# Asking later for the second group's weights, with two parts in flight instead of four

## The chip, the cores and the metric

The kernel runs on one core of a Trainium2 chip. The metric is device time in microseconds (us) for one execution. The engines named below are TensorE (PE, with its weight loads as PEld), VectorE (DVE), ScalarE (ACT), GpSimd (POOL) and SyncE (SP), which here only issues DMAs. Each engine works through its own instructions in program order.

## The reference

A retention layer, then a feed-forward block with the activation h * erf(softplus(h)):

```python
batch, n_heads, seq, head_dim = (8, 8, 576, 64)
scores = scale * np.matmul(q, k.transpose(0, 1, 3, 2))
Dmat = np.where(rel >= 0, gamma[:, None, None] ** rel[None, :, :], 0.0)
attn = np.matmul(scores * Dmat[None], v)
x = attn.transpose(0, 2, 1, 3).reshape(4608, 512)
h = x @ w_in                       # w_in  512 x 2048
sp = np.maximum(h, 0.0) + np.log1p(np.exp(-np.abs(h)))
out = (h * erf(sp)) @ w_out        # w_out 2048 x 512
```

The two weight matrices arrive as 64-bit floats. The kernel reads them as pairs of 32-bit words and rounds them to 32-bit floats itself.

## The kernel before

**Attention.** The 4608 tokens are cut into 36 pieces of 128 tokens, all eight heads at a time. A piece goes through three stages, `transposes` (L303), `scores` (L329) and `outputs` (L342); `attend` (L438) runs the next ones of the list. From piece 8 on, q and k are loaded as 32-row squares (`raw_qs`, `raw_ks`, four or eight DMAs each, L130) and turned by DVE into `qT` and `kT` (L314), which the scores on PE (L335) need. The squares have two buffers: `transposes(i)` asks for q and k of piece i+2, `outputs(i)` asks for the rows of k and v of piece i+3 (`raw_k`, `raw_v`, L144). All these DMAs are issued by SP.

**Feed-forward.** Four pieces make a chunk of 512 tokens, and there are nine chunks. The 2048 inner columns are cut into four groups of 512. That gives 36 pairs (group, chunk), numbered n = 0 to 35, the nine chunks of group 0 first. Both products of a pair are made in a seven-product scheme, so a pair has seven products of PE in `First` (x times w_in, L478) and seven in `Second` (times w_out, L585), besides the first pair, which is computed plainly (L532). Below, Fn and Sn are `firsts[n]` and `seconds[n]`.

**Order.** The main loop (L735) writes out the order of all engines by hand. Its blocks are F1, S0, F2, S1, F3, S2 and so on. Block Fn holds the three products of Fn's `middle`, the two of S(n-1)'s `first` and the two of Fn's `last`. Block Sn holds Sn's `middle` (3), F(n+2)'s `first` (2) and Sn's `last` (2). Between products stand attention stages and single steps of the weight rounding. `run(steps, rounds)` (L696) says how many rounding steps follow each product.

**Weights.** `load_weights` (L224) issues the next part: 128 partitions by 1024 words, 512 KB, as two DMAs of 256 KB for w_in or one of 512 KB for w_out, into one of the four `wraw` buffers. A group has four parts `wa` of w_in and four parts `wb` of w_out. `rounding` (L232) rounds one part in five steps:

1. ACT: absolute value of the high words into the operand tile, and the low words scaled (L246, L247)
2. DVE: a clamp (L251)
3. DVE: a shift (L255)
4. DVE: the sign put back (L259)
5. DVE: a mask (L264); then two operations on POOL (L266, L267), which replace two on DVE outside the first four parts; then, for groups after the first, the next `load_weights`

After the fourth part of `wa` and of `wb` come four more steps, one addition on DVE each (`sums_in`, `sums_out`). A group so takes 48 steps. `most_g` lets a step touch a group only from the group before it on. The operand tiles `wa` and `wb` have two buffers each. Group 1's `wa` is first used by F9's `first`, which stands in block S7, and its `wb` by S9's `first`, in block F10.

Before the change, two parts of group 1 are asked for at block F1 and two at block F2 (L739), so four are in flight, and each finished part asks for the next. Its rounding starts in block S0, with five steps in each block Fn and two in each Sn, and ends in block S6.

Of the kernel before, what the change touches and what calls it, by code (L numbers as in the profile page):

```python
# [54 lines left out]
def kernel(  # L55
# [15 lines left out]
    n_ch = n_tok // TCH  # L71
# [26 lines left out]
    def tt(out, in0, in1, op):  # L98
        nc.vector.tensor_tensor(out=out, in0=in0, in1=in1, op=op)  # L99
# [75 lines left out]
    A11, S3, A12, A22, S1, S2, S4 = range(7)  # L175
    B11, T3, B21, B22, T1, T2, T4 = range(7)
    weights = {}

    def operands(name, g):
        if (name, g) not in weights:  # L180
            shape = [P, 7, 2, GW] if name == "wa" else [P, 7, GP, OH]
            weights[name, g] = wpool.tile(shape, FP32, tag=name, name=name)
        return weights[name, g]
# [40 lines left out]
    def load_weights():  # L224
        part = next(coming, None)
        if part is not None:
            t = wraw.tile([P, 2 * WP], UINT32, tag="wraw", name="wraw")
            for rows, src in part[0]:
                nc.sync.dma_start(out=t[rows].rearrange("p (h f) -> p h f", h=2), in_=src)
            words.append((t, *part[1:]))  # L230

    def rounding():  # L232


        while True:
            while not words or words[0][2] > most_g[0]:
                yield
            t, name, g, slot, j, sums = words.pop(0)
            w = operands(name, g)
            dst = w[:, slot : slot + 2, j, :]  # L240
            pairs = t[:, :].rearrange("p (h f two) -> p h f two", h=2, two=2)
            pairs_f = t[:, :].bitcast(FP32).rearrange("p (h f two) -> p h f two", h=2, two=2)
            low, high = pairs[:, :, :, 0], pairs[:, :, :, 1]
            r_f, high_f = pairs_f[:, :, :, 0], pairs_f[:, :, :, 1]
            a_f, a = dst, dst.bitcast(UINT32)
            nc.scalar.activation(a_f, high_f, AF.Abs)  # L246
            nc.scalar.mul(out=r_f, in_=low, mul=2.0**-52)  # L247
            yield


            nc.vector.tensor_scalar(  # L251
                out=a_f, in0=a_f, scalar1=HIGH_LEAST, scalar2=HIGH_MOST, op0=ALU.max, op1=ALU.min
            )
            yield
            nc.vector.tensor_scalar(  # L255
                out=a, in0=a, scalar1=3, scalar2=0x3FFFFFFF, op0=ALU.logical_shift_left, op1=ALU.bitwise_and
            )
            yield
            nc.vector.scalar_tensor_tensor(  # L259
                out=a, in0=high, scalar=0xC0000000, in1=a, op0=ALU.bitwise_and, op1=ALU.bitwise_or  # L260
            )
            yield

            nc.vector.tensor_scalar(out=high, in0=a, scalar1=0xFF800000, scalar2=None, op0=ALU.bitwise_and)  # L264
            engine = nc.vector if (name, g) == ("wa", 0) else nc.gpsimd
            engine.tensor_tensor(out=r_f, in0=high_f, in1=r_f, op=ALU.mult)  # L266
            engine.tensor_tensor(out=a_f, in0=a_f, in1=r_f, op=ALU.add)  # L267
            if g > 0:
                load_weights()
            yield  # L270
            if sums:
                yield from sums(*(w[:, i] for i in range(7)))

    round_step = rounding()

    def round_weights(n=1):
        for _ in range(n):
            next(round_step, None)
# [155 lines left out]
    def after_chunk(c):  # L434

        return stages.index((outputs, (c + 1) * PC - 1)) + 1

    def attend(upto):  # L438
        while done[0] < min(upto, len(stages)):
            of, i = stages[done[0]]  # L440
            of(i)
            done[0] += 1
# [7 lines left out]
    def store_x(c):  # L450
        nc.sync.dma_start(out=xd[c], in_=x[0, c][:, :n_dc])

    def operands_x(g, c):
        t = x[g, c]
        b11, b12, b21, b22 = (t[:, 2 * d : 2 * d + 2, h * TH : (h + 1) * TH] for d in range(2) for h in range(2))
        t1, t2, t4 = (t[:, n_dc + j, :].rearrange("p (d i) -> p d i", d=2) for j in range(3))
        if g == 0 or c == 0:
            tt(t1, b12, b11, ALU.subtract)
            tt(t2, b22, t1, ALU.subtract)
            tt(b12, b22, b12, ALU.subtract)  # L460
        else:
            tt(t2, b12, b11, ALU.add)
            tt(t1, b22, t2, ALU.subtract)
        if g == 0:
            store_x(c)
        tt(t4, b21, t2, ALU.subtract)
        x[g, c] = {A11: b11, A12: b21, S4: b22, A22: t4, S1: t1, S2: t2, S3: b12}

    class First:
# [3 lines left out]
            self.g, self.c = g, c  # L473

        def product(self, a, acc, start):
            for j in range(GP):
                for d in range(2):
                    nc.tensor.matmul(  # L478
                        acc[:, j * TH : (j + 1) * TH],
                        lhsT=weights["wa", self.g][:, a, d, j * P : (j + 1) * P],  # L480
                        rhs=x[self.g, self.c][a][:, d, :],
                        start=(start and j == 0 and d == 0),
                        stop=(d == 1),
                        skip_group_check=True,
                    )
# [71 lines left out]
        def sums(self, parts=(0, 1)):  # L557
            g11, g21, g12, g22 = (t[:, j] for t in (self.t1, self.t2) for j in range(2))
            s1, s2, s3, s4 = (self.s[:, i, j] for i in range(2) for j in range(2))
            if 0 in parts:  # L560
                tt(s1, g12, g22, ALU.add)
                tt(s2, s1, g11, ALU.subtract)
            if 1 in parts:
                tt(s3, g11, g12, ALU.subtract)
                tt(s4, g21, s2, ALU.subtract)

            self.left = {B11: g11, B21: g21, T2: s2, T3: s3, T1: s1, B22: s4, T4: g22}

    class Second:
# [9 lines left out]
                nc.sync.dma_start(out=self.o, in_=od[self.c])  # L579

        def product(self, b, acc, start):
            left = self.of.left[b]
            for j in range(GP):
                for tp in range(2):
                    nc.tensor.matmul(  # L585
                        acc[:, tp, :],
                        lhsT=left[:, j * TH + tp * P : j * TH + (tp + 1) * P],
                        rhs=weights["wb", self.g][:, b, j, :],
                        start=(start and j == 0 and tp == 0),
                        stop=(j == GP - 1),  # L590
                        skip_group_check=True,
                    )
# [86 lines left out]
    firsts = [First(g, c) for g, c in order]  # L679
    seconds = [Second(f) for f in firsts]  # L680
# [15 lines left out]
    def run(steps, rounds=(), stages=1):  # L696

        for step, _ in enumerate(steps):
            attend(min(done[0] + stages, most[0]))
            round_weights(rounds[step] if step < len(rounds) else 0)  # L700
# [34 lines left out]
    for b, nxt in zip(blocks[1:], blocks[2:] + [None]):  # L735
        n = order.index((b.g, b.c))
        if isinstance(b, First):
            most_g[0] = order[n - 1][0] + 1
            if n in (1, 2):  # L739
                load_weights()  # L740
                load_weights()
            run(b.middle(), (1, 1))
            firsts[n - 1].sums()
            run(seconds[n - 1].first(), (1, 1) if n > 1 else ())
            run(b.last(), (1,) if 1 < n < n_ch else ())
            most[0] = before_chunk(n + 3)
        elif n + 2 < n_s:
            f = firsts[n + 1]
            for step, _ in enumerate(b.middle()):
                attend(min(done[0] + 1, most[0]))  # L750
                if step == 0:
                    f.erf()
                elif step == 1 and n + 2 >= n_ch:
                    operands_x(*order[n + 2])
            if n + 2 < n_ch:
                attend(after_chunk(n + 2))
                operands_x(*order[n + 2])
            run(nxt.first(), (1,))
            f.multiply()
            seconds[n + 1].begin()  # L760
            if n_ch <= n + 3 < n_s:
                load_x(*order[n + 3])
            run(b.last(), (0, 1))
        elif n + 1 < n_s:
            firsts[n + 1].erf()
            seconds[n + 1].begin()
            rest = b.rest()
            for _ in range(3):
                next(rest)
            firsts[n + 1].multiply()  # L770
            run(rest)
            firsts[n + 1].sums((0,))
            first = nxt.first()
            next(first)
            firsts[n + 1].sums((1,))
            run(first)
        else:
            run(b.rest())
# [30 lines left out]
```

## Time and profile before

| | |
|---|---|
| time, median of 6 runs | 1038.26 us (1037.45 to 1038.70) |
| time of the profiled execution | 1038.08 us |
| its span, first to last instruction | 1036.3 us |
| mean granted TensorE clock | 0.998 |
| PE busy / PEld busy | 1016.5 us / 875.1 us |
| DVE / ACT / POOL busy | 675.2 / 387.5 / 125.6 us |
| DMA bytes, mean rate | 167.27 MB, 161 GB/s |

The profiled execution is one of the runs of the median; the 1.8 us by which its time exceeds its span lie before its first and after its last instruction. Busy time of PE includes modelled ends, so that 98% busy doesn't mean PE at its peak; a stall is seen where PE's busy time falls below the length of a window. The scores of the first pieces that use the squares stand at 67 us, those of the last piece at 320 us. Where a number below is the start of an instruction, it is in us from the start of the span.

These are the first products of some blocks on PE, to find the places in the trace:

| first product of | start, us |
|---|---|
| S0 first / F1 last | 80.1 / 88.2 |
| F2 middle / F2 last | 114.9 / 129.0 |
| F3 middle / F3 last | 156.2 / 169.4 |
| F4 first / F4 middle | 188.2 / 198.9 |
| F7 middle / F8 middle | 318.0 / 345.5 |
| F9 first / F9 middle | 363.6 / 370.5 |
| S9 first | 400.0 |

### The profile page before, as it was taken

The page shows a single profiled execution, that of the slowest core. Times are in us where ns is not written, and L with a number is a line of the kernel's source. Part 1 is how long each engine was busy: PE and PEld are TensorE (multiplying, and loading weights), DVE is VectorE, ACT ScalarE, POOL GpSimd, SP SyncE. Part 2 cuts the span into 40 slices and gives each one's busy share as a digit, 9 for nine tenths or more (in the row PEclk, how much of TensorE's full clock was granted, in tenths as well). Part 3 has the DMA queues.
Part 4 walks back from the last instruction along what each step waited for, and adds up shares of the span by engine and source line. Part 5 has one row for each costly group of instructions (what it writes and reads, how often), then busy time and mean ns, then how long its engine had stood idle before and what let it go on. Part 6 is the DMA issues. An engine that isn't in the chain of part 4 may idle for free.

```text
span 1036.3 us, 15904 instructions
## 1 busy us (share of the span) xinstructions
PE 1016.5 (98%) x6322; PEld 875.1 (84%) x6322; DVE 675.2 (65%) x1063; ACT 387.5 (37%) x477; POOL 125.6 (12%) x122
## 2 busy tenths in 40 slices
PE   9899999999999999999999999999999999999998
PEld 7777877778788888888888888888888888888887
DVE  3998967768876645567665656666666655555555
ACT  2353232232343444433434334444443333333332
POOL 2151222321312100100001000100100000000000
PEclk9999999999999999999999999999999999999999
DMA  9989989979984531633274424353333334444433
GB/s 192 203 208 225 252 183 250 226 182 250 225 198 141 182 123 40 240 146 142 65 260 143 168 96 143 143 214 152 122 122 122 122 121 130 132 131 131 127 88 116
DMA packets 148778, 167.27 MB, mean 161 GB/s; under 512 B 97632, under 2 KB 123360, under 8 KB 140640
## 3 DMA queue, kind: packets, MB, share of 16 engines
q1 hardware_dynamic: 147696, 165.47, 56.1%
q8 instruction: 50, 0.82, 0.3%
q10 hardware_dynamic: 1008, 0.79, 0.3%
q14 instruction: 24, 0.20, 0.1%
HBM read 119.02 MB, written 47.19 MB: 160 GB/s over the span
## 4 chain that ended last, share of the span: by engine, by line
PE 81%; DMA 8%; DVE 6%; SPq 3%; issue 1%; ACT 1%; POOL 0%; DVEq 0%; POOLq 0%
PE a L585 22%; PE a L478 21%; PE g L585 11%; PE g L478 11%; PE e L585 5%; PE e L478 5%; DMA raw_ks<-in_k_dram 2%; PE s L335 2%; PE o L353 2%; DMA raw_k<-in_k_dram 2%; SPq L130 1%; DVE t L99 1%; DMA od<-o 1%; SPq L144 1%; DVE x L99 1%; PE o L376 1%
## 5 line engine op out<-in xcount | busy, mean ns | idle before, releaser
L478 PE MATMUL a<-x,wa 128*128 128x256 f32 x1120 | 266.2, 381 | 0.0
L478 PEld LDWEIGHTS a<-x,wa 128*128 128x128 f32 x1120 | 211.7, 190 | 29.3
L585 PE MATMUL a<-wb,s 128*128 128x256 f32 x864 | 205.7, 381 | 0.0
L585 PEld LDWEIGHTS a<-wb,s 128*128 128x128 f32 x864 | 163.1, 190 | 23.4 <-ACT o L599 0.7
L99 DVE TENSOR_TENSOR t<-g,t 128x512 f32<-128x512 f32 x70 | 48.3, 690 | 151.5 <-ACT t L508 113.3
L478 PE MATMUL g<-x,wa 128*128 128x256 f32 x560 | 133.2, 381 | 0.5 <-DVE o L99 0.5
L478 PEld LDWEIGHTS g<-x,wa 128*128 128x128 f32 x560 | 105.8, 190 | 15.6 <-DVE o L99 0.9
L99 DVE TENSOR_TENSOR o<-a,o 128x512 f32<-128x512 f32 x108 | 74.3, 688 | 50.4 <-PE a L585 50.4
L503 ACT COPY t<-a 128x512 f32<-128x512 f32 x35 | 20.5, 586 | 187.5 <-PE a L478 187.5
L99 DVE TENSOR_TENSOR t<-t,s 128x1024 f32<-128x1024 f32 x72 | 88.1, 1264 | 0.0
L266 POOL TENSOR_TENSOR wraw<-wraw 128x512 f32<-128x512 f32 x28 | 29.4, 1051 | 463.5 <-DVE wraw L264 253.9
L547 ACT ACTIVATE s<-t 128x1024 f32<-128x1024 f32 x72 | 72.1, 1048 | 35.5 <-DVE t L99 35.5
L99 DVE TENSOR_TENSOR x<-x 128x512 f32<-128x512 f32 x116 | 77.9, 704 | 1.2
L514 ACT COPY t<-a 128x512 f32<-128x512 f32 x35 | 20.5, 586 | 153.0 <-PE a L478 153.0
L551 ACT ACTIVATE s<-s 128x1024 f32<-128x1024 f32 x72 | 72.1, 1049 | 0.4
L585 PE MATMUL g<-wb,s 128*128 128x256 f32 x288 | 68.6, 381 | 2.3 <-DVE t L99 2.3
L585 PE MATMUL a<-wb,t 128*128 128x256 f32 x288 | 68.6, 381 | 1.1 <-DVE t L99 1.1
L585 PE MATMUL e<-wb,t 128*128 128x256 f32 x288 | 68.6, 381 | 0.0
L585 PE MATMUL g<-wb,t 128*128 128x256 f32 x288 | 68.2, 380 | 0.0
L478 PE MATMUL e<-x,wa 128*128 128x256 f32 x280 | 66.8, 381 | 0.0
L99 DVE TENSOR_TENSOR o<-g,o 128x512 f32<-128x512 f32 x72 | 49.3, 685 | 25.6 <-ACT o L599 20.8
L585 PEld LDWEIGHTS g<-wb,s 128*128 128x128 f32 x288 | 54.3, 190 | 9.9 <-DVE t L99 2.5
(75 smaller groups left out, 1194.6 us busy)
## 6 DMA issues: line engine op xcount, KB each, us to landing
od<-o SPq DMA_DIRECT2D x54, 512.0 KB, 3.3
x<-xd SPq DMA_DIRECT2D x27, 1024.0 KB, 4.9
o<-od SPq DMA_DIRECT2D x27, 1024.0 KB, 4.9
raw_qs<-in_q_dram SPq DMA_DIRECT2D x96, 112.0 KB, 4.8
raw_ks<-in_k_dram SPq DMA_DIRECT2D x96, 112.0 KB, 4.2
xd<-x SPq DMA_DIRECT2D x9, 1024.0 KB, 5.2
raw_k<-in_k_dram SPq DMA_DIRECT2D x64, 128.0 KB, 4.5
raw_v<-in_v_dram SPq DMA_DIRECT2D x64, 128.0 KB, 4.3
```

The costliest lines, as they stand in the source:

```text
L99: nc.vector.tensor_tensor(out=out, in0=in0, in1=in1, op=op)
L130: nc.sync.dma_start(out=t[part * SQ : (part + 1) * SQ, :, at : at + m - SQ], in_=tokens[:, :, d0 : d0 + m - SQ])
L144: nc.sync.dma_start(out=t[r0 : r0 + n, e::2, :], in_=heads.rearrange("h p d -> p h d"))
L266: engine.tensor_tensor(out=r_f, in0=high_f, in1=r_f, op=ALU.mult)
L335: nc.tensor.matmul(ps[e][:, p, :], lhsT=t["kT"][heads[e], p, :], rhs=t["qT"][heads[e], p, :], start=True, stop=True)
L353: nc.tensor.matmul(o[p % 2][heads[(e + p) % 2], p // 2, :], lhsT=t["v"][:, 2 * p + e, :], rhs=t["sT"][:, e, p, :], start=(p < 2), stop=(no ...
L478: nc.tensor.matmul(acc[:, j * TH : (j + 1) * TH], lhsT=weights["wa", self.g][:, a, d, j * P : (j + 1) * P], rhs=x[self.g, self.c][a][:, d, :],
L503: nc.scalar.copy(out=self.t1[:, 1], in_=self.a)
L514: nc.scalar.copy(out=self.t2[:, 0], in_=self.a)
L547: nc.scalar.activation(self.s[:, j], t, AF.Softplus)
L551: nc.scalar.activation(self.s[:, j], self.s[:, j], AF.Erf)
L585: nc.tensor.matmul(acc[:, tp, :], lhsT=left[:, j * TH + tp * P : j * TH + (tp + 1) * P], rhs=weights["wb", self.g][:, b, j, :], start=(sta ...
```

## The change

Group 1's first part is asked for at the end of block F2 and another one at the end of block F3, one each. Each finished part still asks for the next one, so that about two are in flight from then on, through all later groups. Blocks S0, F2 and S1 lose their rounding steps. Blocks F3 on keep five and blocks S2 on two. Blocks S6 to S8 get a third one behind the last product of `middle`, as far as steps are left. Counted by steps: group 0 ends as before in F1; group 1's steps 1 to 24 (`wa`) run from F3 to F6, step 44 (the last part rounded) stands in S7, and steps 45 to 48 (the sums of `wb`) in F9. From group 2 on, the rounding steps stand where they stood. The order of PE's instructions is the same as before. The `rounded` set only serves assertions when the program is built.

```diff
+    rounded = set()
...
             if sums:
-                yield from sums(*(w[:, i] for i in range(7)))
+                for step, _ in enumerate(sums(*(w[:, i] for i in range(7)))):
+                    if step == 3:
+                        rounded.add((name, g))
+                    yield
...
         def product(self, a, acc, start):
+            assert ("wa", self.g) in rounded
...
         def product(self, b, acc, start):
+            assert ("wb", self.g) in rounded
...
             most_g[0] = order[n - 1][0] + 1
-            if n in (1, 2):
+            run(b.middle(), (1, 1) if n != 2 else ())
+            firsts[n - 1].sums()
+            run(seconds[n - 1].first(), (1, 1) if n > 2 else ())
+            run(b.last(), (1,) if 2 < n < n_ch else ())
+            if n in (2, 3):
                 load_weights()
-                load_weights()
-            run(b.middle(), (1, 1))
-            firsts[n - 1].sums()
-            run(seconds[n - 1].first(), (1, 1) if n > 1 else ())
-            run(b.last(), (1,) if 1 < n < n_ch else ())
             most[0] = before_chunk(n + 3)
         elif n + 2 < n_s:
...
                 elif step == 1 and n + 2 >= n_ch:
                     operands_x(*order[n + 2])
+                elif step == 2 and n_ch - 4 < n < n_ch:
+                    round_weights()
...
-            run(nxt.first(), (1,))
+            run(nxt.first(), (1,) if n > 1 else ())
             f.multiply()
...
-            run(b.last(), (0, 1))
+            run(b.last(), (0, 1) if n > 1 else ())
```

## The prediction, made before the run

> **What bounds the kernel now.** I read the share of each engine first, then the busy time by stretches, then what PE waited for, then SP's issues around those waits.
>
> ```profile
> PE 1016.5 (98%) x6322; PEld 875.1 (84%) x6322; DVE 675.2 (65%) x1063; ACT 387.5 (37%) x477; POOL 125.6 (12%) x122
> ...
> 84.00:133.00 49.00, 49.00 (x483) 40.02 (x480) 40.18 (x69) 15.42 (x20) 10.37 (x11) 1.00 1.04 228
> 133.00:177.00 44.00, 42.01 (x417) 34.05 (x417) 32.25 (x57) 12.30 (x16) 8.24 (x9) 1.00 0.95 214
> 177.00:214.00 37.00, 35.21 (x345) 28.65 (x342) 29.32 (x50) 10.43 (x14) 10.50 (x10) 1.00 1.05 240
> 214.00:262.00 48.00, 45.73 (x429) 37.45 (x426) 35.49 (x61) 14.20 (x19) 10.38 (x10) 1.00 0.86 205
> 262.00:316.00 54.00, 54.00 (x484) 44.09 (x486) 42.42 (x70) 20.67 (x27) 15.00 (x15) 1.00 0.94 205
> 316.00:350.00 34.00, 33.51 (x242) 28.33 (x239) 21.19 (x39) 12.76 (x17) 5.74 (x6) 1.00 0.44 140
> 350.00:1030.00 680.00, 680.00 (x3151) 598.77 (x3150) 410.08 (x615) 271.01 (x318) 38.23 (x33) 1.00 0.40 138
> ```
>
> Columns of the stretches: from and to, length, busy us of PE, PEld, DVE, ACT, POOL, granted clock, DMA share, GB/s. PE is the bound almost everywhere. From 350 us on it has no gap, so nothing can be gained there. Between 84 us, where the first load that the change moves is issued, and 350 us, PE lacks 1.99 + 1.79 + 2.27 + 0.49 = 6.54 us. That is the whole pot. The DMAs are busy at 0.86 to 1.05 until 316 us. What PE waited for in 84 to 350 us (total, times, longest):
>
> ```profile
> PE s L335 <- DVE kT L314: 3.8, 4, 1.8
> PE g L585 <- DVE t L99: 2.3, 2, 1.7
> PE g L478 <- DVE o L99: 0.5, 1, 0.5
> ```
>
> Four gaps before scores, waiting for turned k, make 3.8 us. One by one on PE's timeline they are 0.98 us at 140.86 (piece 16), 0.19 at 158.34 (18), 0.83 at 176.29 (20) and 1.79 at 187.06 (21). Behind the 1.8 stands this, on SP and in the chain of waits:
>
> ```profile
> 175.46 0.63 SPq L229 DMA_DIRECT2D wraw<-in_moe_w_out_dram  x1
> 176.19 1.99 SPq L130 DMA_DIRECT2D raw_qs<-in_q_dram  x4
> 178.27 3.65 SPq L130 DMA_DIRECT2D raw_ks<-in_k_dram  x4
> ...
> 187.87 1.81 SPq L130 DMA_DIRECT2D raw_ks<-in_k_dram  x4
> ```
>
> ```profile
> 175.46 6.13 DMA wraw<-in_moe_w_out_dram
> 181.59 0.02 issue
> 181.60 4.10 DMA raw_ks<-in_k_dram
> ```
>
> The same four issues of k take 3.65 us behind a weight part and 1.81 without one. The chain says why: the fourth waited until the weight part, eight DMAs before it in SP's order, had landed. A part costs the loads behind it twice, by bandwidth and by this wait. Piece 16 has the same picture:
>
> ```profile
> 125.72 2.60 SPq L229 DMA_DIRECT2D wraw<-in_moe_w_in_dram  x4
> 128.42 1.97 SPq L130 DMA_DIRECT2D raw_qs<-in_q_dram  x4
> 130.73 4.79 SPq L130 DMA_DIRECT2D raw_ks<-in_k_dram  x4
> ```
>
> **The change, part by part.** PE's order is unchanged and no instruction is added or dropped, so only gaps count. *Loads.* From 84 us to the end of the attention loads SP issued ten parts, and now issues six. Counted in the new order, the parts ahead of the q and k loads are: piece 16 four before, none now; pieces 18 and 20 five, then none and one; 21 six, one; 23 six, three; 25 seven, three; 33 nine, six. At 217 GB/s (the five stretches to 316 us, weighted) a part of 524288 bytes is 2.4 us. SP runs late in this stretch: the q squares of 21 could go out once piece 19's were turned at 163.7, and go out at 176.19. So five parts less, up to 12 us, is real lead for pieces 16 to 21, and the 3.79 us of their gaps should go. I take 3.6; at least 2.5, if 16 and half the rest go.
>
> *The two DVE gaps* (1.66 at 223.45 and 0.61 at 261.86) wait for an addition `t` that DVE reached late, since just before it had idled 2.04 + 1.43 us for q and k of piece 25, and 2.15 + 0.90 us for piece 29. With four parts less ahead, that idling shrinks by up to 9.6 us less the 3.8 that PE then runs earlier. I take 1.3 of the 2.27; bounds 0 and 2.27.
>
> *The gap at 347.88* (0.49) is DVE's queue, no DMA: behind the four operand sums stand a rounding step of 0.69 (L259), then the addition and two multiplications, and only then `o`, which frees the PSUM tile. Counting steps, that slot now holds an ACT step, and block S6's third step puts 0.42 (L264) earlier. Gain 0.2; bounds -0.4 and 0.49.
>
> *The moved steps.* S0, F2 and S1 lose nine steps, and S6 to F9 get them. In S7 the new steps are 0.42 (L255) and 0.69 (L259) on DVE, which idles 1.10 and 0.42 us there, at 367.35 and 370.73; cost nothing, 0.5 if that cover is gone. The weights' use is safe: step 24 falls in F6, 39 us before F9 needs it, and the sums end by 379 us, before S9's middle needs them at 407. POOL's two operations (1.04 + 1.29) come along, and POOL has 10 of 49 us busy. SP's waits at L229 for freed buffers (113.8 us for DVE after 350) go too, worth nothing where PE has no gap.
>
> *The new place.* Two parts, four DMAs of w_in, now stand between v of piece 22 and q of piece 23. SP reached that place at 191.91. At piece 16 the time from the first of four such DMAs to turned k was 125.72 to 140.80, 15.1 us. Piece 23's scores started at 204.11 without a gap, and will be wanted 3.8 us earlier, at 200.3. If SP is earlier by 3.8 only, the four go out at 188.1, k is ready at 203.2, and PE waits 2.9 us. If it is 7 us or more ahead, of the 12 that five parts give, PE waits nothing. I take the middle, 1.4; bounds 0 and 2.9.
>
> A load asked for late can also hold ACT: part 2's first step stands behind F4's first copy, at 190.18 + 0.59 before. With issue at 188.1 and 6.9 us to land (the four at 125.72 took 4.9 to 7.5), ACT stands until 195. Its next copy, at 196.07 before, had 5.30 us of idling ahead of it, and would be late by some 4 us, with DVE's clamp behind it by 2. I count that inside the same 2.9, as it is the same lateness.
>
> The trace shows the first two parts issued at 84.37 to 86.28, landed by 93.38 and first used at 105.53: they lie idle for 12 us, so there is room to ask later, and only part 2 comes near its use. The Trainium skill speaks against the change here: "DMA: Bandwidth & Descriptors", rules for kernel authors, says to issue a DMA early and wait for it late. By that rule alone asking later could only lose, and the sum would be zero or a loss.
>
> Sum: 3.6 + 1.3 + 0.2 - 1.4 = 3.7 us off the profiled execution's 1038.08 (span 1036.3 and 1.8 around it), that is 1034.4. The median of the runs is 0.18 higher than that execution, so 1034.6. Bounds: 3.79 + 2.27 + 0.49 = 6.55 gained, 1031.7; and 2.5 - 2.9 - 0.4 - 0.5 = 1.3 lost, 1039.6.
>
> **The rivals.** *All gaps go* (1031.7): five parts of lead outrun what PE gains, 12 us against 3.8, and at piece 23 three parts still do, 7.2 against 3.8. Against it: DVE is 72 to 82% busy there, and gaps closed early make later ones tighter.
>
> *The wait moves to piece 23* (about 1037.4): SP gets ahead only as far as PE does, because its other issues wait for buffers and results in order; 3.6 gained, 2.9 lost there, the rest unchanged. For it: the block of four is the very one that stalled piece 16. Against it: SP ran 12 us behind its buffers at piece 21.
>
> *Slower: the block of four arrives with no lead at all.* Issued at 191.9 it makes k of piece 23 ready at 207.0, 6.7 us after the wanted 200.3, and the late data carry the DVE gap at 223 along; 3.6 gained, 6.7 lost, 1038.26 + 3.1 = 1041.4. It decides once the issue comes later than 188.1 + 0.7 + 2.1 = 190.9, where loss exceeds gain by over 2.1. Against it: that needs five parts' transfers to have cost SP nothing, which the 3.65 against 1.81 denies.
>
> *It doesn't do what it says*: if attention loads, not weights, fill the DMAs to the same lateness, gaps stay, 1038. The rows of piece 21 speak against it; it belongs with no change.
>
> **How the numbers follow.** About 0.2%, 2.1 us, is what a measurement tells from no change: faster is below 1036.2, slower above 1040.3. Forecast (1034.6, own range 1032.6 to 1036.2) 0.42; all gaps go 0.20; moved to piece 23, or nothing done, 0.26; slower 0.12. That gives faster 0.62, same 0.26, slower 0.12. The range 1031.5 to 1038.8 leaves out the slower rival and the edge of no change.
>
> **What would show it.** Right: gaps at pieces 16, 20 and 21 gone; a gap of 0 to 2.9 at piece 23; PE busy 44.0 of 44 in the stretch that ends at 177; 350 on still without gaps. Wrong: gaps there in spite of four q and k issues at 1.8 us (then DVE was the cause), a long ACT wait at L246 for its part before F4's middle, or new gaps at S7 and F9.

## The result and the profile after

The changed kernel takes 1035.69 us (median of 18 runs, 1033.71 to 1038.21), beside 1038.47 for the kernel before (38 runs, those of the same chips included). The ratio is 0.9974, with a 95% interval of 0.9968 to 0.9981: faster by 0.26%, some 2.8 us. The forecast was 1034.6 us, with a range of 1031.5 to 1038.8, and faster with a chance of 0.62.

The profiled execution took 1036.4 us, with a span of 1034.6 us, 1.7 less than before. These are the same stretches of the changed kernel (from and to, length, busy us of PE, PEld, DVE, ACT, POOL, granted clock, DMA share, GB/s) and what PE waited for in 84 to 350 us (total, times, longest). Lines of the code have moved: the loads of weights are now L230, the turning L318, scores L339, the products L483 and L591, the mask of the rounding L265 and POOL's two operations L267 and L268.

```profile
133.00:177.00 44.00, 44.00 (x429) 35.90 (x428) 33.70 (x60) 14.25 (x19) 9.14 (x10) 1.00 0.88 209
177.00:214.00 37.00, 37.00 (x347) 30.25 (x347) 29.35 (x47) 11.57 (x17) 8.00 (x9) 1.00 1.04 228
214.00:262.00 48.00, 45.20 (x435) 36.83 (x434) 33.41 (x60) 16.24 (x22) 11.03 (x12) 1.00 0.88 204
262.00:316.00 54.00, 54.00 (x510) 44.18 (x509) 45.98 (x76) 15.81 (x21) 11.50 (x12) 1.00 0.97 220
316.00:350.00 34.00, 31.96 (x198) 27.12 (x197) 19.73 (x32) 14.04 (x20) 7.32 (x6) 1.00 0.35 117
350.00:1030.00 680.00, 680.00 (x3152) 598.75 (x3150) 413.92 (x622) 271.97 (x320) 42.30 (x36) 1.00 0.42 140
```

```profile
PE g L483 <- DVE o L99: 2.0, 1, 2.0
PE s L339 <- DVE kT L318: 1.5, 1, 1.5
PE g L591 <- DVE t L99: 1.3, 1, 1.3
```

PE lacks 2.80 us in 214 to 262 and 2.04 in 316 to 350, together 4.84 instead of 6.54. The 1.70 us between the two sums is the 1.7 between the spans. But it is not the same gaps that were there before. The 3.79 us at pieces 16, 18, 20 and 21 are gone to the last tenth, and so is the 0.61 at 261.86. The wait for the addition `t` that cost 1.66 costs 1.34 (at 219.30). Two things came in: 1.46 us at 239.98, before the scores of piece 27, and the gap at F8's middle has grown from 0.49 to 2.04 us (at 346.13). The chain before piece 27's scores, with the last of its k squares waiting for a weight DMA to land:

```profile
228.09 5.26 DMA wraw<-in_moe_w_in_dram
...
233.37 5.24 DMA raw_ks<-in_k_dram
...
239.98 1.16 PE s L339 x16
```

SP at the place of the two parts, in the changed kernel:

```profile
184.21 2.48 SPq L230 DMA_DIRECT2D wraw<-in_moe_w_in_dram  x4
186.79 1.96 SPq L130 DMA_DIRECT2D raw_qs<-in_q_dram  x4
188.85 4.62 SPq L130 DMA_DIRECT2D raw_ks<-in_k_dram  x4
```

Again the four issues of k take 4.62 us behind weights. SP came there early enough: k of piece 23 was turned by 199.34, and PE took it at 200.29, without a gap. DVE, then PE:

```profile
198.24 1.10 DVE L318 STREAM_TRANSPOSE kT<-raw_ks 128x512 f32<-128x512 f32 x1 [0.88 <-DMA raw_ks<-in_k_dram]
```

```profile
200.29 1.16 PE L339 MATMUL s<-qT,kT 64*128 64x128 f32 x16
```

One of the prediction's signs of being wrong did come: ACT waited 4.08 us for part 2 before F4's middle.

```profile
191.02 0.69 ACT L247 ACTIVATE wa<-wraw 128x512 f32<-128x512 f32 x1 [4.08 <-DMA wraw<-in_moe_w_in_dram]
```

It cost nothing: ACT's next copy started at 192.24, 3.83 us earlier than before (196.07), and PE was 3.8 us earlier there too.

### The profile page after: what moved, and what is told of

Same layout as the page of the kernel before. It is cut to its first block, busy times and chain, and to the rows that moved or that the text cites. A ratio compares the mean times of both kernels' runs of the same rounds, so it can differ in the third digit from the quotient of the medians.

```text
span 1034.6 us, 15920 instructions
## 1 busy us (share of the span) xinstructions
PE 1015.2 (98%) x6322; PEld 872.8 (84%) x6322; DVE 679.0 (66%) x1063; ACT 387.7 (37%) x477; POOL 124.0 (12%) x122
## 4 chain that ended last, share of the span: by engine, by line
PE 87%; DVE 5%; DMA 3%; SPq 2%; ACT 1%; issue 1%; DVEq 0%; ACTq 0%
PE a L591 23%; PE a L483 22%; PE g L483 12%; PE g L591 11%; PE e L591 6%; PE e L483 5%; PE s L339 3%; PE o L357 2%; SPq L144 2%; PE o L380 1%; DMA wraw<-in_moe_w_in_dram 1%; DVE x L99 1%; PE o L368 1%; DMA raw_ks<-in_k_dram 1%; DVE sT L99 1%
## 5 line engine op out<-in xcount | busy, mean ns | idle before, releaser
L483 PE MATMUL a<-x,wa 128*128 128x256 f32 x1120 | 266.1, 381 | 0.0
L483 PEld LDWEIGHTS a<-x,wa 128*128 128x128 f32 x1120 | 211.8, 190 | 29.3
L591 PE MATMUL a<-wb,s 128*128 128x256 f32 x864 | 205.7, 381 | 0.0
L591 PEld LDWEIGHTS a<-wb,s 128*128 128x128 f32 x864 | 163.1, 190 | 23.4 <-ACT o L605 0.7
L483 PE MATMUL g<-x,wa 128*128 128x256 f32 x560 | 133.2, 381 | 2.0 <-DVE o L99 2.0
L483 PEld LDWEIGHTS g<-x,wa 128*128 128x128 f32 x560 | 105.8, 190 | 17.1 <-DVE o L99 2.4
L267 POOL TENSOR_TENSOR wraw<-wraw 128x512 f32<-128x512 f32 x28 | 29.7, 1062 | 434.6 <-DVE wraw L265 173.3
L591 PE MATMUL g<-wb,s 128*128 128x256 f32 x288 | 68.6, 381 | 1.3 <-DVE t L99 1.3
L591 PE MATMUL a<-wb,t 128*128 128x256 f32 x288 | 68.6, 381 | 0.3 <-DVE t L99 0.3
L591 PE MATMUL e<-wb,t 128*128 128x256 f32 x288 | 68.6, 381 | 0.0
L591 PE MATMUL g<-wb,t 128*128 128x256 f32 x288 | 68.2, 380 | 0.0
L483 PE MATMUL e<-x,wa 128*128 128x256 f32 x280 | 66.8, 381 | 0.0
L99 DVE TENSOR_TENSOR sT<-s,cst 128x512 f32<-128x512 f32 x72 | 46.2, 683 | 25.6 <-PE s L339 25.5
```

The costliest lines, as they stand in the source:

```text
L483: nc.tensor.matmul(acc[:, j * TH : (j + 1) * TH], lhsT=weights["wa", self.g][:, a, d, j * P : (j + 1) * P], rhs=x[self.g, self.c][a][:, d, :],
L591: nc.tensor.matmul(acc[:, tp, :], lhsT=left[:, j * TH + tp * P : j * TH + (tp + 1) * P], rhs=weights["wb", self.g][:, b, j, :], start=(sta ...
```

## The experiments

**The loads, or the rounding steps?** The change moves both. e1 takes the kernel before and only halves the parts in flight; the first two are still asked for at F1, and every rounding step stays where it was:

```diff
-            if n in (1, 2):
+            if n == 1:
                 load_weights()
                 load_weights()
```

> The kernel before, with two parts asked for at block F1 and none at F2: two in flight, rounding steps where they were. If the place and number of the loads made the gain: the gap at piece 16 (0.98 us) goes, that at piece 20 goes or shrinks, that at piece 21 stays at 1 us or more, since a part still stands just ahead of its q; 1036.5 to 1037.7 us. If the moved rounding steps made the gain: as before, 1038.5, with the gap at piece 16 still there.

e2 does the other half alone, on the changed kernel:

```diff
+            if n in (1, 2):
+                load_weights()
+                load_weights()
             run(b.middle(), (1, 1) if n != 2 else ())
...
-            if n in (2, 3):
-                load_weights()
```

> The changed kernel, with two parts asked for at the start of F1 and two at the start of F2, as before; only the rounding steps are moved. If the loads made the gain: piece 16 keeps its gap of about 1 us, pieces 20 and 21 lose theirs only as far as finished parts ask later, and the time is 1036.5 to 1038. If the moved steps made it: as the changed kernel, 1035.7, no gap at piece 16.

e1 took 1035.27 us, ratio 0.9971 (0.9958 to 0.9984). e2 took 1038.64, ratio 1.0004 (0.9993 to 1.0015). So the two parts fewer in flight bring the gain without the later start and without the moved steps, and the moved steps bring nothing by themselves. PE's waits in 84 to 350 us, first e1, then e2:

```profile
PE g L585 <- DVE t L99: 1.6, 2, 1.2
PE o L353 <- POOL raw_v L301: 0.8, 1, 0.8
PE g L478 <- DVE o L99: 0.5, 1, 0.5
```

```profile
PE s L339 <- DVE kT L318: 2.7, 3, 1.6
PE g L591 <- DVE t L99: 2.3, 2, 1.2
PE g L483 <- DVE o L99: 2.0, 1, 2.0
PE o L357 <- POOL raw_v L305: 1.2, 2, 0.8
```

e1 has no gap before scores left; a wait of 0.8 us for `raw_v`, which POOL weighs, is new. e2 has 1.61 us at piece 16 (140.64), as expected of the loads, and already shows the 2.0 at F8's middle. Both times lie outside what was expected of the loads: e2's above, with 8.4 us that PE lacks in 84 to 350 us (6.5 before), e1's below. I had expected e1 to keep a gap at piece 21, since its two DMAs of w_in stand just ahead of that piece's q. It has none: SP issued that q at 171.85 in e1, 176.19 before, 4.3 us earlier. Already at piece 16's q it was 4.0 us earlier (124.41, 128.42 before), so the delay before piece 21 had begun with the four DMAs in front of piece 16.

**What of a weight part hurts?** e5 leaves the kernel's loads where they were before, as many of them, and moves an eighth of the bytes for groups 1 to 3:

```diff
-            t = wraw.tile([P, 2 * WP], UINT32, tag="wraw", name="wraw")
+            t = raws[count[0] % 4]
+            count[0] += 1
+            m = WP if part[2] == 0 else 64
             for rows, src in part[0]:
-                nc.sync.dma_start(out=t[rows].rearrange("p (h f) -> p h f", h=2), in_=src)
+                nc.sync.dma_start(out=t[rows].rearrange("p (h f) -> p h f", h=2)[:, :, :m], in_=src[:, :, :m])
```

> The kernel before, with as many weight DMAs at the same places, but for groups 1 to 3 each moves only 64 of every 512 words (the operands of these groups are then made from older words, so the output changes); four fixed buffers stand in for the pool. If a weight part hurts by what it moves and how long it keeps its place among SP's eight: gaps at pieces 16, 20 and 21 together under 0.8 us instead of 3.6, 1035 us or less. If it hurts by SP's time to issue it: gaps of some 3 us as before, 1038.

1031.71 us, ratio 0.9929 (0.9911 to 0.9947). Of PE's gaps after 84 us one is left:

```profile
PE g L482 <- DVE o L99: 0.5, 1, 0.5
```

So it is the transfer of the part, not SP's time to issue it: the four weight DMAs ahead of piece 16 took SP 2.79 us to issue, 2.60 before. With the bytes goes both what they take of the DMAs' rate and how long they hold their place among SP's eight; this run doesn't part the two.

To part them, e8 (on e3, below) and e9 (on e1) gave the weight DMAs of groups 1 to 3 to ACT's queue:

```diff
-                nc.sync.dma_start(out=t[rows].rearrange("p (h f) -> p h f", h=2), in_=src)
+                queue = nc.sync if part[2] == 0 else nc.scalar
+                queue.dma_start(out=t[rows].rearrange("p (h f) -> p h f", h=2), in_=src)
```

> The kernel of e3 (the changed kernel with the early third step), with the weight DMAs of groups 1 to 3 issued by ACT and not by SP. If the waits for a landed weight part in SP's order made the remaining gap at piece 27: it goes or falls under 0.7 us from 1.9, and 1033 us. If the bandwidth they share does, or ACT's time for issuing comes in: gap of 1 us or more there, 1034 us or more.

> The kernel of e1 (two in flight, steps where they were) with the weight DMAs of groups 1 to 3 issued by ACT. SP's order decides: no gap of scores, raw_v gap at 197 us gone, 1034 us. Bandwidth or ACT's issuing decides: 1035.3 or more.

Both are far slower: e8 1061.4 us, ratio 1.0212 (1.0190 to 1.0234), and e9 1068.88, ratio 1.0283 (1.0262 to 1.0305). By their times the second reading of both holds, in which ACT's issuing comes in, but neither had this size or this cause. In e9, first what SP waited for most in 60 to 350 us (total, times, longest), then SP and ACT around 340 us:

```profile
SPq L130 <- DMA wraw<-in_moe_w_in_dram: 26.5, 4, 10.5
```

```profile
330.82 14.03 SPq L130 DMA_DIRECT2D raw_ks<-in_k_dram  x8
```

```profile
340.41 1.21 ACTq L230 DMA_DIRECT2D wraw<-in_moe_w_in_dram  x2
```

SP stood from 334.05 to 344.54 before the last of k's eight squares, and went on when ACT's first DMA, issued at 340.41, had landed at 344.52. In the trace the DMAs of SP and ACT take eight completion semaphores (the counters that say that a transfer has landed) in turn, and this square and ACT's DMA have the same one. So SP waits for a transfer that ACT, still behind in its own queue, has not even issued. This shows that the wait for a place among the eight can hold SP for 10 us by itself where the DMA in that place is issued late; what part of the 3.8 us it made in the kernel before, and what part the rate, stays open.

**The gap at F8's middle.** DVE and POOL in the changed kernel:

```profile
337.85 0.42 DVE L265 TENSOR_SCALAR wraw<-wb 128x512 uint32<-128x512 uint32 x1
338.18 4.43 DVE L99 TENSOR_TENSOR x<-x 128x512 f32<-128x512 f32 x4
342.53 0.68 DVE L99 TENSOR_TENSOR t<-e,t 128x512 f32<-128x512 f32 x1
```

```profile
338.40 1.36 POOL L267 TENSOR_TENSOR wraw<-wraw 128x512 f32<-128x512 f32 x1 [16.42 <-ACT wb L247]
339.84 1.62 POOL L268 TENSOR_TENSOR wb<-wb,wraw 128x512 f32<-128x512 f32 x1
```

and the same four sums in the kernel before:

```profile
341.14 2.61 DVE L99 TENSOR_TENSOR x<-x 128x512 f32<-128x512 f32 x4
```

The third rounding step of S6 is by its number the mask, the step that releases POOL's two operations. They run beside the operand sums, which take 1.82 us longer. With the mask of 0.42 ahead of the sums and the step of 0.69 gone from behind them, 1.82 + 0.42 - 0.69 = 1.55 us, which is what the gap grew by. e3 puts the third step where DVE idles, behind the middle's first product; e4 leaves POOL's two operations out for this one part.

```diff
                 if step == 0:
                     f.erf()
+                    if n_ch - 4 < n < n_ch:
+                        round_weights()
...
-                elif step == 2 and n_ch - 4 < n < n_ch:
-                    round_weights()
```

> The changed kernel, with the third rounding step of blocks S6 to S8 behind the first product of the middle, where DVE idled 6.3 us, and not behind the third. If the gap of 2.0 us at F8's middle came from POOL's two operations running beside the four operand sums on DVE: the sums take 2.6 us again instead of 4.4, the gap falls to 0.5 or less, 1034.2 us. If it was only one more step of 0.42 us in DVE's queue: the gap falls to about 1.6, 1035.3.

```diff
-            engine.tensor_tensor(out=r_f, in0=high_f, in1=r_f, op=ALU.mult)
-            engine.tensor_tensor(out=a_f, in0=a_f, in1=r_f, op=ALU.add)
+            if (name, g, slot, j) != ("wb", 1, B11, 1):
+                engine.tensor_tensor(out=r_f, in0=high_f, in1=r_f, op=ALU.mult)
+                engine.tensor_tensor(out=a_f, in0=a_f, in1=r_f, op=ALU.add)
```

> The changed kernel without POOL's two operations for the one part that is masked in block S6 (the low words of that part are not added, which changes the output); every DVE step stays in its place. If POOL stretched the operand sums: 2.6 us for the four, the gap at F8's middle 0.5 or less, 1034.2 us. If DVE's own queue was too long: sums and gap as in the changed kernel, 4.4 and 2.0 us, 1035.7.

e3 took 1034.14 us, ratio 0.9961 (0.9949 to 0.9973), and has no gap there. e4 took 1033.32, ratio 0.9957 (0.9941 to 0.9974), and has 0.21 left. DVE in e4, with the mask still in its place, and POOL in e3, now well before the sums at 338.63:

```profile
339.50 0.42 DVE L265 TENSOR_SCALAR wraw<-wb 128x512 uint32<-128x512 uint32 x1
339.83 2.62 DVE L99 TENSOR_TENSOR x<-x 128x512 f32<-128x512 f32 x4
```

```profile
332.17 1.04 POOL L267 TENSOR_TENSOR wraw<-wraw 128x512 f32<-128x512 f32 x1 [9.39 <-issue]
333.29 1.29 POOL L268 TENSOR_TENSOR wb<-wb,wraw 128x512 f32<-128x512 f32 x1
```

With nothing changed on DVE, the sums are back at 2.62 without POOL. So it is POOL's operations that stretch them.

**Versions that may beat both.** e10 moves the S blocks' step in e1 in the same way as e3:

```diff
                 if step == 0:
                     f.erf()
+                    round_weights()
...
-            run(nxt.first(), (1,))
+            run(nxt.first())
```

> The kernel of e1 with the rounding step of the S blocks behind the first product of the middle instead of the first product of the next First. The step of 0.69 us then stands in DVE's idle time before F8, and the gap of 0.48 us at F8's middle should go: 1034.8 us. If that gap is the multiplications alone, it stays and so does the time, 1035.3.

The gap at F8's middle went, as expected. The time, 1036.40 us on a chip where the kernel before had 1039.97, ratio 0.9968 (0.9953 to 0.9982), can't be told from e1's. So I ran the candidates beside the changed kernel on one chip. r1 is the changed kernel, r2 is e3, r3 is e10, and e11 is e10 with the two DMAs of a w_in part issued one rounding step apart.

> The changed kernel itself, on the same chip as the next three, for a direct comparison: 0.9974 of before, with gaps of some 5 us on PE between 84 and 350 us, 2.0 of them at F8's middle.

> The kernel of e3 beside the changed kernel. If POOL's collision cost 2 us of the time and not only of one profile: 1.5 to 2 us below r1, no gap at F8's middle. If what is closed there opens elsewhere: within 0.7 us of r1.

> The kernel of e10 beside the changed kernel. If PE's gaps set the time (0.9 us after 84 us in its profile, 4.8 in that of the changed kernel): 3 us or more below r1. If the runs differ by something else: within 1 us of r1.

```diff
+                if m and part[2] > 0:
+                    later.append((t, rows, src))
+                else:
+                    nc.sync.dma_start(out=t[rows].rearrange("p (h f) -> p h f", h=2), in_=src)
...
         for _ in range(n):
+            load_later()
             next(round_step, None)
```

> The kernel of e10, with the two DMAs of a w_in part issued one rounding step apart, so that they don't stand together in SP's order. If the pair ahead of q and k makes what gaps are left at pieces 21 to 27: none of scores over 0.3 us, 0.3 to 0.9 us below r3. If other DMAs (xd, od) make them: as r3.

| | median, us | ratio to before | 95% interval |
|---|---|---|---|
| r1, the changed kernel | 1035.25 | 0.9965 | 0.9954 to 0.9977 |
| r2, third step early | 1033.88 | 0.9943 | 0.9928 to 0.9958 |
| r3, two in flight, step moved | 1034.97 | 0.9957 | 0.9941 to 0.9973 |
| e11, one DMA at a time | 1035.42 | 0.9968 | 0.9953 to 0.9983 |

r2 is 1.4 us below r1, somewhat less than the 2.0 of the gap; in r2's profile that gap is gone, but a wait of 0.9 us for `t` stands there that r1's doesn't have. Eleven of r1's twelve runs lie above the highest of r2's six (1034.36), though the two intervals meet. So the step's place costs about 1.4 us, a third of the 4.4 us that the change gains on this chip. The changed kernel with that step moved has the lowest median of the versions here that compute the same output, but its interval overlaps that of r3. r3 against r1 is not the 3 us that the first profile of e10 promised; its second profile has 3.2 us of gaps after 84 us instead of 0.9. e11 is inconclusive: the scores of piece 27 still wait 0.44 us, more than the 0.3 expected, and its time doesn't differ from r3's beyond the intervals.

## Why the prediction was right, and where it was not

*The four gaps before scores* (3.6 taken of 3.79): right, all 3.79 gone, and by what the prediction named. e1 and e2 put it on the loads, e5 on their transfer. What I didn't separate beforehand is which of the loads: fewer in flight is enough. The rule quoted against the change, to issue early, would have had e1 lose or gain nothing, as it asks later for two of the parts; it gained (ratio 0.9971).

*The two DVE gaps* (1.3 taken of 2.27): 0.93 came. The one at 261.86 went, the other shrank to 1.34. In r1, the same kernel again, the other is gone too, so one profile doesn't settle this term.

*The new place* (1.4 lost at piece 23): the size agrees by luck, since the wait came at another place. At piece 23 SP was 191.91 - 184.21 = 7.7 us ahead, as much as the prediction wanted for no wait, and there was none. The wait of 1.46 us (2.02 in r1) came at piece 27, behind the next pair of w_in DMAs. SP's lead over the kernel before, compared by the first q square, shrinks from 7.9 us (piece 21) to 5.1 (23), 3.8 (25) and 3.5 (27). PE itself then ran 3.8 us earlier or more, so from piece 25 on SP had nothing to spare. The prediction added up bytes and let the lead stay at three or four parts' worth; it was not kept.

*The gap at 347.88* (gain 0.2, bounds -0.4 and 0.49): this is the step that failed. It grew by 1.55 us, outside its bounds, and again in r1 (2.03) and in e2 (2.04). I counted the steps right: an ACT step where a DVE step of 0.69 had been, a DVE step of 0.42 before the sums. I priced the mask at DVE's 0.42 and let POOL's two operations "come along" at no cost, since POOL was idle. What they cost is not POOL's time but DVE's: 1.82 us on four sums. The trace before could have told: its multiplications `t<-t,s` of 128x1024 ran at a median of 1217 ns alone, and the five that ran beside a POOL operation for over 0.2 us at 2061.

*The moved steps in S7 and F9* (0): right, no gap there, and none after 350 us.

*The slower rival* needed the block of four to arrive with no lead; it arrived with 7.7 us. *All gaps go* gave 1031.7. e5, where the transfers shrink, closes all but one and takes 1031.71, but that the numbers agree is luck: on its chip the kernel before took 1039.97, so it gained 8.3 us, more than the 6.1 of the gaps that its profile closes.

In the sum, 3.79 + 0.93 - 1.46 - 1.55 = 1.71 us, the difference of the two spans and less than half of the 3.7 forecast. The medians differ by 2.8. The profiled execution before lay 0.4 us below its median and the one after 0.7 above, which is the rest; what set these two apart from the other runs is not shown. So that the measured 1035.69 lies near the forecast 1034.6 is in part luck, and the stated range was wide enough to hold no change as well.

## What to carry to other kernels

Where one queue issues everything and PE just keeps up with it, the number of large prefetches in flight is a knob by itself: halving it gave the whole gain here (e1), with one new wait of 0.8 us. A DMA that isn't urgent delayed the urgent ones behind it by its transfer, not by its issue (e5). When a step is moved to another place of a schedule written by hand, look up what it releases on other engines, and whether that runs beside an instruction that PE waits for.

## What the runs showed of the hardware

**POOL slows some of DVE's operations, not all.** In the trace before, `x<-x` of 128x512 takes 684 ns alone, and the operations on scores in PSUM (`sT`, 33 of them for over 0.2 us beside a POOL operation) take 680 ns with and 681 without. In the changed kernel the four sums at F8's middle (shortest, median, longest in ns) are

```profile
L99 DVE TENSOR_TENSOR x<-x x4: 679/1050/1774, 338.2 to 341.9; 128x512 f32<-128x512 f32 x4
```

The first of them, begun 0.22 us before POOL's first operation, took 686 ns, and POOL's 1.36 us instead of 1.04; the next two, begun while POOL worked, took 1415 and 1774. The Trainium skill, "SBUF — State Buffer", section on who interferes with whom, says the same: an operation of DVE with two SBUF inputs and one of GpSimd that reads SBUF exclude each other, whichever starts first.

**A gap of 2 us can cost 3.7.** r1's profiled execution took 1040.09 us, nearly 5 above its median. It has four stretches at half clock: one at 32 us, near where the profile of the kernel before has one too (33.38), and three more. The first of the three follows a gap of 1.90 us at 82.75; r2 has the same gap at 82.61 and no such stretch. First r1, then r2:

```profile
78.00:83.00 5.00, 2.80 (x13) 1.78 (x11) 5.00 (x7) 1.17 (x2) 1.65 (x1) 1.00 0.91 293
83.00:87.00 4.00, 3.85 (x35) 3.47 (x34) 3.97 (x7) 0.00 (x0) 0.00 (x0) 0.57 1.18 214
```

```profile
78.00:83.00 5.00, 2.80 (x12) 1.64 (x11) 5.00 (x7) 1.17 (x2) 1.56 (x1) 1.00 1.02 326
83.00:87.00 4.00, 3.85 (x45) 3.29 (x46) 3.96 (x7) 0.00 (x0) 0.00 (x0) 1.00 1.20 208
```

The clock falls to 0.57 in the mean and 35 matmuls run instead of 45. By the records of the clock each such stretch lasts 3.413 us at 0.5, so it takes 1.7 us of work. The other two in r1 follow gaps of 2.02 (piece 27) and 2.03 (F8's middle), and three times 1.7 is about the excess over the median. The profile of the changed kernel has the same 2.04 at F8's middle and kept its clock, so the length of the gap alone doesn't decide.

What decides is where the gap falls on a fixed grid. In r1 the stretches begin at 32.21, 83.41, 240.42 and 349.65 us, which are 15, 46 and 32 times 3.413 apart, and in each of the 14 traces all half-clock stretches lie on one such grid, at an offset that differs from execution to execution. I took PE's idle time in every window of these grids that ran at full clock, from 25 us on (4097 windows). All 20 windows with 1.92 us or more of idle were followed by half clock, 3 of the 9 with 1.62 to 1.92, and none of the 4068 with less. In r1 the gap of 2.03 at F8's middle left 1.99 in one window; in the changed kernel's profile a border of the grid (345.71) cut its 2.04 into 1.61 and 0.43. The Trainium skill, "TensorE: Matmul & The Clock Gate", part 1, tells of a free-running window of 3413 ns, which agrees. Its section "Why this matters for your kernels" asks only for no gaps over about 3 us; here a gap of 1.90 was enough.
